# A gradient intermediate kept out of DRAM, transposes moved to other stages, and stores moved to another engine, in a fused forward and backward of linear attention and SwiGLU

## The chip, the cores and the metric

The kernel runs on one core of a Trainium2 chip. The metric is the device time of one execution in microseconds (us). Each time below is a median of several executions, and each ratio has a 95% interval. A single profile is one execution; in this case executions of one kernel differ by up to 3%, so a profile is used to see where time goes and the medians and ratios to say how much.

## The reference

One block on an input of 2048 rows and 640 columns in bfloat16, with 32 heads of 20 columns and a feed-forward width of 1728. The kernel returns the output and the gradients of x, wqkv, wo, w_gate, w_up and w_down for a given gradient of the output.

```python
def _A_ref(x, wqkv, wo):                        # linear attention
    q, k, v = ...                               # from x @ wqkv, per head
    phi = lambda t: where(t > 0, t + 1, exp(t)) + 1e-6
    pq, pk = phi(q), phi(k)
    kv  = einsum("bhsd,bhse->bhde", pk, v)
    z   = einsum("bhsd->bhd", pk)
    num = einsum("bhqd,bhde->bhqe", pq, kv)
    den = einsum("bhqd,bhd->bhq", pq, z)[..., None] + 1e-6
    return merge_heads(num / den) @ wo

def _B_ref(x, w_gate, w_up, w_down):            # SwiGLU
    return (silu(x @ w_gate) * (x @ w_up)) @ w_down

h   = x + _A_ref(layernorm(x), wqkv, wo)
out = h + _B_ref(layernorm(h), w_gate, w_up, w_down)
# ... and the vector-Jacobian product of out with grad_out
```

## The kernel before

Everything is done in row tiles of 128 rows. The parts that the argument needs, in order of time:

* **The h1 stage.** h1 = x + attention, its layer norm (`hn`) and its transpose (`hnT`). The products dm = grad_out @ w_down^T for the feed-forward gradient are computed between the others; those of three of the four column groups of w_gate and w_up are stored in DRAM.
* **Four column groups** of 448, 448, 448 and 384 columns, called groups 0 to 3. In each, g and u are computed, then m = silu(g)*u and the gradients dgate and dup (`dd`), then the weight gradients (`ps_dw`, copied out of PSUM as `dwev`). Each tile of `dd` is transposed by SP into one of three staging buffers `stg` and stored in DRAM by GpSimd. I call this the staging ring.
* **The dhn stage** reads the transposed tiles back (`cols`), **the dxn stage** makes the gradients of q and k, and the last stage makes the output from m transposed.

```python
# ... in column group g, for each pair of row tiles:
for c in range(2):                                       # the staging ring
    stg = small.tile([P, 7, P], BF16, name="stg", tag="stg", bufs=3)
    nc.sync.dma_start_transpose(out=stg[:, :GK[g], :], in_=ddt[:, tt + c, 0:2 * w])
    nc.gpsimd.dma_start(out=scr_dT[t + c, :, KO[g]:KO[g] + GK[g], :], in_=stg[:, :GK[g], :])
# ... (cut) the dm of the next group is loaded from DRAM, wgT transposed by SP
def dw(parts, copy, first=False):                        # weight gradients
    ps = mm("ps_dw")
    # ... (cut) 16 matmuls for each part
    ev = fw("dwev")
    copy(out=ev[:, :len(parts), :w], in_=ps[:, :len(parts), :w])
    for c, (_, _, dst) in enumerate(parts):
        nc.gpsimd.dma_start(out=dst[:, GO[g]:GO[g] + w], in_=ev[:, c, :w])
# ... (cut) last stage: m is transposed where it is used
def load_mT(t):
    if t % 4 == 0:
        mTs[t // 4] = strips.tile([P, 4, FT, P], BF16, name="mT", tag="S")
    nc.sync.dma_start_transpose(out=mTs[t // 4][:, t % 4], in_=scr_m[t * P:(t + 1) * P, :])
```

## Time and profile before

| | before |
|---|---|
| median of six runs beside the changed kernel | 852.02 us (847.09 to 854.31) |
| profiled span | 848.7 us |
| PE busy | 827.0 us, 97% |
| PE's two long waits | 5.4 us (at 254 us), 5.0 us (at 664 us) |

How to read it: a busy PE at its pace leaves only the waits to win, and the prediction shows them. One more line matters later, which the prediction did not use. It is from the page's part on DMA: the packets, the bytes and the mean rate over the span.

```profile
DMA packets 304402, 175.78 MB, mean 207 GB/s; under 512 B 250528, under 2 KB 290000, under 8 KB 304336
```

The five DMA queues of the page add up to 88% of the time of the 16 DMA engines. So the DMA engines are the second-busiest thing in this kernel, although no wait of PE shows it directly.

### The profile page before, as it was taken

The page shows a single profiled execution, that of the slowest core. Times are in us where ns is not written, and L with a number is a line of the kernel's source. Part 1 is how long each engine was busy: PE and PEld are TensorE (multiplying, and loading weights), DVE is VectorE, ACT ScalarE, POOL GpSimd, SP SyncE. Part 2 cuts the span into 40 slices and gives each one's busy share as a digit, 9 for nine tenths or more (in the row PEclk, how much of TensorE's full clock was granted, in tenths as well). Part 3 has the DMA queues.
Part 4 walks back from the last instruction along what each step waited for, and adds up shares of the span by engine and source line. Part 5 has one row for each costly group of instructions (what it writes and reads, how often), then busy time and mean ns, then how long its engine had stood idle before and what let it go on. Part 6 is the DMA issues. An engine that isn't in the chain of part 4 may idle for free.

```text
span 848.7 us, 14059 instructions
## 1 busy us (share of the span) xinstructions
PE 827.0 (97%) x5509; PEld 529.8 (62%) x5509; DVE 417.5 (49%) x840; ACT 297.8 (35%) x422; POOL 193.7 (23%) x352
## 2 busy tenths in 40 slices
PE   8999999999979999999999999999999799999997
PEld 6666655654535455555556777777777577777775
DVE  6978844786008603920750145577850466521111
ACT  5983433293109304800831222232221133332000
POOL 2330111222142241214213311111101122112322
PEclk9999999999999999999999999999999999999999
DMA  9999978999999995999488679567499899899692
GB/s 297 194 294 286 273 191 248 217 179 242 249 213 227 219 232 148 203 239 227 114 230 240 246 216 194 152 158 174 94 217 262 169 179 172 156 200 253 183 210 87
DMA packets 304402, 175.78 MB, mean 207 GB/s; under 512 B 250528, under 2 KB 290000, under 8 KB 304336
## 3 DMA queue, kind: packets, MB, share of 16 engines
q1 hardware_dynamic: 267808, 86.35, 53.6%
q0 software_dynamic: 19072, 70.79, 26.8%
q10 hardware_dynamic: 17456, 17.75, 7.5%
q8 instruction: 43, 0.70, 0.4%
q14 instruction: 23, 0.19, 0.1%
HBM read 53.72 MB, written 64.01 MB: 139 GB/s over the span
## 4 chain that ended last, share of the span: by engine, by line
PE 60%; DMA 16%; DVE 12%; issue 8%; POOL 1%; ACT 1%; SPq 0%; DVEq 0%; POOLq 0%; ACTq 0%
PE ps_dw L521 14%; PE ps_dxn L746 8%; PE ps_o L794 7%; PE ps_dm L315 7%; DMA dwd<-scr_dwdT 6%; PE ps_dhn L120 4%; DMA stg<-dd 4%; PE ps_kq L120 3%; PE ps_dwqk L120 3%; PE ps_y L120 3%; PE ps_a L120 3%; DMA scr_dT<-stg 2%; PE ps_dk L120 2%; PE pg L461 2%; PE pu L466 2%
## 5 line engine op out<-in xcount | busy, mean ns | idle before, releaser
L120 PE MATMUL ps_dhn<-wgT,cols 128*128 128x320 bf16 x864 | 119.5, 299 | 0.0
L521 PE MATMUL ps_dw<-dd,hn 128*128 128x448 bf16 (+1 forms) x640 | 118.8, 346 | 0.0
L120 PEld LDWEIGHTS <-cols 128*128 128x128 bf16 x864 | 84.5, 98 | 32.9
L521 PEld LDWEIGHTS <-hn 128*128 128x128 bf16 x640 | 62.6, 98 | 54.2
L523 DVE CAST dwev<-ps_dw 128x896 bf16<-128x896 f32 (+3 forms) x12 | 10.9, 908 | 140.3 <-PE ps_dw L521 82.9
L523 ACT CAST dwev<-ps_dw 128x896 bf16<-128x896 f32 (+1 forms) x20 | 17.5, 879 | 166.5 <-PE ps_dw L521 139.3
L493 POOL DMA_DIRECT2D scr_dT<-stg x64 | 34.6, 541 | 169.2 <-DMA stg<-dd 163.7
L461 PE MATMUL pg<-wgu,hnT 128*128 128x448 bf16 (+1 forms) x320 | 65.5, 352 | 6.2 <-DVE dwev L523 5.4
L466 PE MATMUL pu<-wgu,hnT 128*128 128x448 bf16 (+1 forms) x320 | 63.6, 346 | 0.0
L794 PE MATMUL ps_o<-wd,mT 128*128 128x320 bf16 x448 | 62.6, 299 | 0.0
L315 PE MATMUL ps_dm<-wdT,dh2T 128*128 128x448 bf16 (+1 forms) x320 | 62.0, 346 | 0.0
L521 PE MATMUL ps_dw<-m_s,dh 128*128 128x448 bf16 (+1 forms) x320 | 60.7, 346 | 0.9 <-DVE m_s L488 0.9
L746 PEld LDWEIGHTS <-ring 128*128 128x128 bf16 x480 | 47.0, 98 | 18.2
L794 PEld LDWEIGHTS <-mT 128*128 128x128 bf16 x448 | 43.8, 98 | 17.0
L461 PEld LDWEIGHTS <-hnT 128*128 128x128 bf16 x320 | 31.7, 99 | 34.7 <-issue 7.4
L746 PE MATMUL ps_dxn<-wqkvT,ring 128*128 128x320 bf16 x320 | 51.3, 299 | 0.0
L521 PEld LDWEIGHTS <-dh 128*128 128x128 bf16 x320 | 31.3, 98 | 28.3 <-issue 1.4
L466 PEld LDWEIGHTS <-hnT 128*128 128x128 bf16 x320 | 31.4, 98 | 27.2 <-issue 0.2
L120 PE MATMUL ps_kq<-wqk,xnT 128*128 128x320 bf16 x320 | 47.5, 305 | 0.8 <-ACT xnT L242 0.8
L315 PEld LDWEIGHTS <-dh2T 128*128 128x128 bf16 x320 | 31.3, 98 | 25.1
L120 PEld LDWEIGHTS <-xn_r 128*128 128x128 bf16 x320 | 31.8, 99 | 18.1 <-issue 5.2
L797 DVE TENSOR_TENSOR h1r<-ps_o,h1r 128x640 bf16<-128x640 f32 x15 | 12.4, 824 | 57.0 <-PE ps_o L794 54.1
(158 smaller groups left out, 1257.6 us busy)
## 6 DMA issues: line engine op xcount, KB each, us to landing
cols<-scr_dT POOLq DMA_DIRECT2D x7, 1728.0 KB, 8.6
scr_dT<-stg POOLq DMA_DIRECT2D x48, 224.0 KB, 3.3
scr_m<-m_s POOLq DMA_DIRECT2D x12, 448.0 KB, 5.1
scr_dm<-dmst ACTq DMA_DIRECT2D x16, 224.0 KB, 3.2
dm_s<-scr_dm ACTq DMA_DIRECT2D x2, 1792.0 KB, 12.4
out_dram<-dwev POOLq DMA_DIRECT2D x30, 112.0 KB, 4.6
scr_dT<-stg POOLq DMA_DIRECT2D x16, 192.0 KB, 3.0
scr_xn<-xn SPq DMA_DIRECT2D x4, 640.0 KB, 5.1
```

The source lines that it names most:

```text
L120: nc.tensor.matmul(ps[:, ci, :320], lhsT=lhs(k), rhs=rhs(k, n0, n1), start=(start and k == 0), stop=(stop and k == n - 1))
L315: nc.tensor.matmul(ps[:, c, :w], lhsT=dh2T[:, kt, (t + c) * P:(t + c + 1) * P], rhs=wdT[g // 2][:, kt, o:o + w], start=(kt == 0), stop=(kt ...
L461: nc.tensor.matmul(pg[:, c, :w], lhsT=hnT[:, kt, (t + c) * P:(t + c + 1) * P], rhs=wg[:, kt, 0:w], start=(kt == 0), stop=(kt == DT - 1))
L466: nc.tensor.matmul(pu[:, c, :w], lhsT=hnT[:, kt, (t + c) * P:(t + c + 1) * P], rhs=wg[:, kt, w:2 * w], start=(kt == 0), stop=(kt == DT - 1))
L493: nc.gpsimd.dma_start(out=scr_dT[t + c, :, KO[g]:KO[g] + GK[g], :], in_=stg[:, :GK[g], :])
L521: nc.tensor.matmul(ps[:, c, :w], lhsT=lhs(t), rhs=rhs(t), start=(t == 0), stop=(t == ST - 1))
L523: copy(out=ev[:, :len(parts), :w], in_=ps[:, :len(parts), :w])
L746: nc.tensor.matmul(ps[:, ci, :320], lhsT=lhs[:, i, :], rhs=rhs[:, i, n0:n1], start=(k == 0 and i == 0), stop=(k == 2 and i == DT - 1))
L794: nc.tensor.matmul(pss[ci][:, ci, :320], lhsT=mT[:, t % 4, j, :], rhs=wd[:, j, n0:n1], start=(j == 0), stop=(j == FT - 1))
L797: nc.vector.tensor_tensor(out=half(h1r[:]), in0=row(ps), in1=half(h1r[:]), op=ALU.add)
```

## The change

The intent, as its author put it: no dm through DRAM; late weights, phi(k) and half of m transposed into DRAM while the DMA engines idle; VectorE in emission order in the backward half. The core of the diff, with cuts:

```diff
-    scr_dm, scr_dm_v = dram_tm("scr_dm", F)
+    scr_wgT = dram.tile([P, 13, D], BF16, name="scr_wgT")
+    scr_mT = dram.tile([ST, P, 7, P], BF16, name="scr_mT")
+    scr_pkT = dram.tile([ST, P, DT, P], BF16, name="scr_pkT")
...  # W2 is transposed ahead of the h1 loop, through the staging buffers
+        for i in range(DT):
+            w2t = stage()[:, :DT, :]
+            nc.sync.dma_start_transpose(out=w2t, in_=W2[:, i, :])
+            nc.gpsimd.dma_start(out=mat_v(scr_W2T)[:, :, i * P:(i + 1) * P], in_=w2t)
...  # dm of groups 2 and 3 is made in PSUM where it is used
+                if g < 2:
+                    dmv = dm_t[g][:, t:t + 2, :w]
+                else:
+                    pdm = mm("pdm")
+                    dm_mm(pdm, wdT, t, g)
+                    dmv = pdm[:, :, :w]
...  # more work for the ring, placed between the weight gradients
+        def tr_m_dram(t):
+            stg = stage()
+            nc.sync.dma_start_transpose(out=stg[:], in_=scr_m[t * P:(t + 1) * P, 0:7 * P])
+            nc.gpsimd.dma_start(out=scr_mT[t], in_=stg[:])
+            elif g == 2:
+                side = [(tr_wgT_dram, (gg, kt)) for gg in (2, 3) for kt in range(DT)]
+                side += [(tr_m_dram, (t,)) for t in range(0, 8)]
+            else:
+                load_cols(0, act_load)
+                act_load(wgT[1][:], scr_wgT[:])
+                side = [(tr_m_dram, (t,)) for t in range(8, ST)]
...  # weight-gradient stores
-                    nc.gpsimd.dma_start(out=dst[:, GO[g]:GO[g] + w], in_=ev[:, c, :w])
+                    nc.scalar.dma_start(out=dst[:, GO[g]:GO[g] + w], in_=ev[:, c, :w])
...  # dhn stage: phi(k) transposed into DRAM; its first plain loads come before the store of GT
+            if t < ST:
+                stg = stage()
+                nc.sync.dma_start_transpose(out=stg[:, :DT, :], in_=scr_pk[t * P:(t + 1) * P, :])
+                nc.gpsimd.dma_start(out=scr_pkT[t], in_=stg[:, :DT, :])
...  # last stage: half of m comes ready from DRAM
-            nc.sync.dma_start_transpose(out=mTs[t // 4][:, t % 4], in_=scr_m[t * P:(t + 1) * P, :])
+            nc.gpsimd.dma_start(out=mTs[t // 4][:, t % 4, 0:7], in_=scr_mT[t])
+            nc.sync.dma_start_transpose(out=mTs[t // 4][:, t % 4, 7:FT], in_=scr_m[t * P:(t + 1) * P, 7 * P:FT * P])
```

## The prediction

> **What bounds the kernel now.** I read the busy table first, then the list of waits of the matmul engine, then the timeline around its two long waits, then the chain that ended last. The busy table and the clock line of the slices:
>
> ```profile
> PE 827.0 (97%) x5509; PEld 529.8 (62%) x5509; DVE 417.5 (49%) x840; ACT 297.8 (35%) x422; POOL 193.7 (23%) x352
> PEclk9999999999999999999999999999999999999999
> ```
>
> PE is busy 97% of 848.7 us. A busy PE need not be at its pace, so I checked that in the chain: ten matmuls of 448 columns take 1.89 us and ten of 320 take 1.36 us wherever they follow each other, and every stage runs so. What is left to win is only the time in which PE stands. The list of PE's waits, whole (total us, times, longest):
>
> ```profile
> PE pg L461 <- DVE dwev L523: 5.4, 1, 5.4
> PE ps_dwqk L120 <- DVE tk L731: 5.0, 1, 5.0
> PE ps_t L241 <- DVE xn L237: 2.0, 2, 1.1
> PE ps_warm L271 <- POOL ident masks.py:199: 1.4, 1, 1.4
> PE ps_dw L521 <- DVE m_s L488: 0.9, 2, 0.7
> PE pg L461 <- DMA hnT<-hn: 0.8, 1, 0.8
> PE ps_kq L120 <- ACT xnT L242: 0.8, 1, 0.8
> ```
>
> Two waits matter, and each slows the work after it. In the timeline of PE (start, length, idle before):
>
> ```profile
> 254.16 3.74 PE L461 MATMUL pg<-wgu,hnT 128*128 128x448 bf16 x10 [5.40 <-DVE dwev L523]
> 664.50 5.82 PE L120 MATMUL ps_dwqk<-dq,xn_r 128*128 128x320 bf16 x32 [5.01 <-DVE tk L731]
> ```
>
> Ten such pg matmuls take 2.05 us elsewhere and 32 such dwqk 4.51, so 1.7 and 1.3 us more go to a clock that is halved after the pause. The first wait is a queue: GpSimd issues the transposed dgate/dup tiles in order, each waiting for its transpose, and the weight-gradient stores stand behind the last of them. At 249 to 258 us it sends fourteen of them one after the other; until then their SBUF buffers, and so the PSUM, stay full. The timeline of GpSimd there:
>
> ```profile
> 248.58 0.54 POOL L493 DMA_DIRECT2D scr_dT<-stg  x1 [4.82 <-DMA stg<-dd]
> 249.11 0.54 POOL L525 DMA_DIRECT2D scr_dwdT<-dwev  x1
> 249.65 2.13 POOL L525 DMA_DIRECT2D out_dram<-dwev  x4
> ```
>
> Ahead of it is a staging ring of three buffers, transposed by SP and emptied by GpSimd. SP's timeline in column groups 0 and 1, then SP's longest wait:
>
> ```profile
> 193.29 50.34 SPq L492 DMA_TRANSPOSE stg<-dd  x16
> 261.86 48.18 SPq L492 DMA_TRANSPOSE stg<-dd  x16
> ```
>
> ```profile
> SPq L492 <- DMA scr_dT<-stg: 79.8, 37, 5.7
> ```
>
> The second wait is a load of phi(k) that GpSimd issued only at 651.99, behind a store, and that took almost 10 us to land.
>
> **What the Trainium skill says.** "TensorE: Matmul & The Clock Gate", Back-to-back issue gap, gives N/2.4 + 2.5 ns per warm matmul: 189 ns for 448 columns, 136 for 320. The trace agrees (1.89 and 1.36 us per ten): PE cannot go faster at this work. Its section What's actually happening has the clock halved for about 3.4 us after an idle window; the trace agrees with the 1.7 and 1.3 us above. "DMA: Bandwidth & Descriptors", Anatomy of one DMA, says that DMA engines do not wait on semaphores, the issuing sequencer does before it dispatches. The trace agrees: GpSimd stood, and everything behind. The same page, Issuing engines are not separate DMA queues: moving an issue to another engine saves no bandwidth, so the ring's pace does not change by that.
>
> **The change, part by part.**
> 1. *PE.* The dm products of column groups 2 and 3 (80 matmuls of 448 and 80 of 384: 15.1 + 13.0 = 28 us) move from the h1 stage into the backward groups. The number of matmuls is the same. Worth: 0 by itself.
> 2. *No dm in DRAM.* Out go 24 stores of 192 or 224 KB and three loads of 1.5 to 1.8 MB (11 to 14 us each to land). While such a load was under way the ring stood: at 288 to 300 us and 363 to 372 us two transposes took about 9 us. Without it I read from SP's issues in groups 1 and 2 before those loads (261.86 to 288.31, 337.18 to 363.56) a pace of 26 us per 10, 2.6 us per tile instead of 2.8 to 3.3. DVE reads dm of two groups from PSUM in two of its seven products. It needs 824 ns for 640 columns from PSUM against 491 from SBUF, so some 1.15 us for 896 instead of 0.62: per pair of row tiles 5 x 0.54 + 2 x 1.15 = 5.0 us beside 3 x 1.89 = 5.67 us of PE. Hidden.
> 3. *Weight-gradient stores issued by ACT.* They no longer stand behind the ring on GpSimd. This should take away the 5.4 + 1.7 us.
> 4. *phi(k) loaded early, from the staging buffers; phi(k) transposed in the idle stage; DVE in emission order.* In the changed order of GpSimd the first two phi(k) loads now stand before the stores of GT and of dwqk. This should take away 5.0 + 1.3 us.
> 5. *Small ones:* w2t leaves the path of hnT and of the ring (0.8 us), and DVE is less behind at the end of groups (0.9).
> Sum that can go: 5.4 + 1.7 + 5.0 + 1.3 + 0.8 + 0.9 = 15.1 us, or 1.8%. More there is not: the other waits are the start, and the last 5.3 us after PE are untouched.
> 6. *Added:* 10 wgT, 16 m and 16 phi(k) tiles go through the ring and DRAM, about 8.4 MB written and read back. They are not on PE, but they lengthen the ring: 16 + 18 steps in group 2, 16 + 8 in group 3.
>
> **The rivals: what takes the place of the waits.**
> *(a) ACT now stands instead of GpSimd.* In the order of the changed kernel with its waits, DMAs of SP and of ACT share eight completion semaphores in turn, and each issue waits for the user before it. So ACT's stores wait for SP's transposes, and ACT evicts PSUM in the same order. In group 1 the last stores wait for the load of the last w_gate/w_up slice, which waits for five transposes, a load, and five more. From the start of that group: first tile at 1.9 + 3 x 0.92 + 7 x 0.54 = 8.5 us; 15 steps of 2.6 = 39; five wgT transposes and landing 13 to 15 (11.45 us in the same place before, plus 3); load issue 1; five more 12 to 13; issue and landing 6. Sum 80 to 83 us. PE comes there after 30.3 + 45.4 = 75.7 us, and PSUM gives it some 4.7 more: 80.4. **So 0 to 3 us of standing, and every 0.1 us of the ring's step is 1.5 us.** At the old step of 3.2 it would be 10.
> *(b) The same in group 2.* The last store waits for ring step 32: first tile at 10.1, 31 steps of 2.6 to 2.8, 4 to land: 95 to 101 us, against 90.8 + 4.1 = 94.9 on PE. 0 to 6 us.
> *(c) The second column load of the next stage.* GpSimd issues it after all 24 ring stores of group 3, and cols(0), wgT and pqs (1.8 + 2.1 + 2.6 MB) load meanwhile; two such loads slowed the ring by 20 us before. I expect the issue some 83 us after the start of the group and the landing 9 to 15 later; PE needs it at 92. 0 to 6 us; before, it landed at 481.80 for a start at 484.4.
> *(d) The h1 stage becomes DVE's.* PE now spends 2.3 us per row tile there instead of 3.0, DVE also about 2.3. 0 to 3 us, mostly hidden by PSUM.
> *(e) Nothing takes the place.* Then the time is 852 - 15 = 837. For it speaks that the DMA bytes fall on the stages with least of them; against it that (a) to (c) are all within a few us of binding.
>
> **Range and chances.** Middle values: (a) 2, (b) 2, (c) 3, (d) 1, halved clock after them 1: 9 us. 852 - 15 + 9 = **846 us**. The low end is (e), 837, where a new wait everywhere is absent. For the high end, a ring at its old step gives 10 in (a), about 8 in (b) and less in (c), 22 in all: 859. Faster by over 2% needs less than 835, more than all that I count: 4%. Slower by over 2% needs over 869, that is 32 us of new waits: 6%.
>
> **What will show it.** The 5.4 us wait for dwev and the 5.0 us wait for tk are gone from PE's list, PE's busy us stay near 827, and DVE's products with dm from PSUM take 1.1 to 1.2 us. SP's 16 ring transposes in group 1 take 38 to 42 us. If (a) holds, PE's list has new waits of its first pg and pu matmuls in groups 2 and 3 on ACT's dwev, and ACT waits there for DMAs of the wgu, wgT or stg tiles. If (c) holds, ps_dhn waits for cols. The prediction is wrong upward if the ring's step stays above 3 us or DVE's fixed order makes it wait in the last half, and downward if the ring runs at 2.4 or less and nothing new appears.

## The result, and the profile after

| | before | after |
|---|---|---|
| median of six runs | 852.02 us | 880.12 us (868.85 to 886.08) |
| ratio | | 1.0301, interval 1.0231 to 1.037 |
| profiled span | 848.7 us | 876.0 us |

A ratio here is the mean time of one kernel's fast runs over the mean time of the other's fast runs of the same rounds, so it is not quite the ratio of the medians. The changed kernel is 3% slower, and the prediction was wrong: 880 us lies far outside its range.

The page of the changed kernel: the busy table, the clock by slices, and the DMA line.

```profile
PE 835.8 (95%) x5509; PEld 532.4 (61%) x5509; DVE 433.4 (49%) x840; ACT 284.4 (32%) x406; POOL 205.1 (23%) x366
PEclk9999989999999999997999899999899999999999
DMA packets 292483, 181.76 MB, mean 207 GB/s; under 512 B 239840, under 2 KB 276512, under 8 KB 292288
```

PE has the same 5509 matmuls but is busy 8.8 us longer: this is halved clock. The mean clock that PE was granted is 0.981 against 0.992 before, and the clock line has slices below 9 where before it had none. The transfers have 6 MB more.

PE's list of waits in the changed kernel (total us, times, longest), its seven longest:

```profile
PE pg L474 <- ACT dwev L546: 7.0, 2, 6.9
PE ps_dhn L122 <- DMA cols<-scr_dT: 6.2, 1, 6.2
PE ps_dhn L122 <- ACT dwev L546: 6.1, 1, 6.1
PE ps_a L122 <- DVE xr L424: 5.5, 1, 5.5
PE ps_dp L122 <- DMA dh1T<-dh: 2.6, 1, 2.6
PE ps_t L245 <- DVE xn L241: 2.0, 2, 1.1
PE pu L479 <- ACT m_s L497: 1.6, 1, 1.6
```

Both waits of before are gone. In their place stand five others of more than 2 us. The sum closes within 1 us: new are 7.0 + 6.2 + 6.1 + 5.5 + 2.6 + 1.6 us, 0.9 us for a tile `ring<-dq` and 0.7 us for h1r, together 30.6 us; PE's busy time adds 8.8; gone are 5.4 + 5.0 + 0.8 = 11.2. That makes 28.2 us, and the spans differ by 27.3.

The wait at the end of group 2, in the chain that ended last (start, length, what):

```profile
388.74 4.80 DMA stg<-scr_m
...
395.11 4.96 DMA scr_mT<-stg
...
400.08 4.91 DMA stg<-scr_m
...
405.01 0.02 ACTq L552
```

Right after it ACT empties the PSUM of the weight gradients and PE goes on at 406.40. The reader sees one staging buffer going round: an m tile is transposed in 4.8 us, stored in 5.0, and only then does the next m tile take the buffer. ACT's store waits for that next tile, although it has nothing to do with it. In the program of the changed kernel, DMAs issued by SP and by ACT share eight completion semaphores in turn, so an issue waits for the earlier DMA that holds its semaphore. ACT's next eviction (its copy of finished sums out of PSUM) stands behind the store, and PE behind the eviction. The ring in groups 2 and 3, in SP's timeline (start, length):

```profile
315.56 40.02 SPq L510 DMA_TRANSPOSE stg<-dd  x16
355.67 29.53 SPq L456 DMA_TRANSPOSE stg<-wgu  x10
387.42 22.82 SPq L462 DMA_TRANSPOSE stg<-scr_m  x8
413.98 49.63 SPq L510 DMA_TRANSPOSE stg<-dd  x16
463.70 29.25 SPq L462 DMA_TRANSPOSE stg<-scr_m  x8
```

The ring of group 2 ends at 410 us, while PE stops at 399.5, a few tiles into group 3. In group 3 the ring ends at 493; PE is through with the group at 482.

The wait in the h1 stage, in GpSimd's timeline:

```profile
119.19 1.74 POOL L413 DMA_DIRECT2D scr_W2T<-stg  x2 [10.99 <-DMA stg<-yk]
120.97 0.24 POOL L133 TENSOR_SCALAR lnv<-mv 128x1 f32<-128x1 f32 x1
121.29 0.57 POOL L134 TENSOR_TENSOR rstd<-lnv,nhalf 128x1 f32<-128x1 f32 x1
```

GpSimd stands 11 us on the last transposed tiles of W2, with the small operations of the layer norm behind them in its order; PE stands for them from 117 us.

### The profile page after: what moved, and what is told of

Same layout as the page of the kernel before. It is cut to its first block, busy times and chain, and to the rows that moved or that the text cites. A ratio compares the mean times of both kernels' runs of the same rounds, so it can differ in the third digit from the quotient of the medians.

```text
span 876.0 us, 14086 instructions
## 1 busy us (share of the span) xinstructions
PE 835.8 (95%) x5509; PEld 532.4 (61%) x5509; DVE 433.4 (49%) x840; ACT 284.4 (32%) x406; POOL 205.1 (23%) x366
## 2 busy tenths in 40 slices
DMA packets 292483, 181.76 MB, mean 207 GB/s; under 512 B 239840, under 2 KB 276512, under 8 KB 292288
## 3 DMA queue, kind: packets, MB, share of 16 engines
q1 hardware_dynamic: 258400, 85.96, 51.3%
q0 software_dynamic: 20496, 78.87, 30.5%
## 4 chain that ended last, share of the span: by engine, by line
PE 54%; DMA 23%; DVE 11%; SPq 5%; issue 3%; ACT 2%; POOL 1%; ACTq 0%; DVEq 0%; POOLq 0%
PE ps_dhn L122 12%; PE ps_dxn L784 7%; PE ps_o L832 6%; DMA stg<-dd 5%; PE ps_dw L544 5%; PE ps_dwqk L122 4%; PE ps_kq L122 3%; PE ps_y L122 3%; DMA scr_dT<-stg 2%; PE ps_dk L122 2%; PE pg L474 2%; PE pu L479 2%; PE pdm L313 2%; SPq L581 2%; PE ps_dm L313 2%
## 5 line engine op out<-in xcount | busy, mean ns | idle before, releaser
L122 PE MATMUL ps_dhn<-wgT,cols 128*128 128x320 bf16 x864 | 124.5, 307 | 12.3 <-DMA cols<-scr_dT 6.2
L122 PEld LDWEIGHTS <-cols 128*128 128x128 bf16 x864 | 86.4, 100 | 48.7 <-DMA cols<-scr_dT 6.6
L784 PE MATMUL ps_dxn<-wqkvT,ring 128*128 128x320 bf16 x320 | 51.3, 299 | 0.9 <-DMA ring<-dq 0.9
L501 DVE TENSOR_TENSOR m_s<-m_s,dd 128x896 bf16<-128x896 bf16 (+1 forms) x32 | 19.3, 603 | 49.7 <-ACT m_s L497 49.7
L495 ACT ACTIVATE dd<-pg 128x896 bf16<-128x896 f32 (+1 forms) x32 | 28.6, 893 | 36.6 <-PE pg L474 34.4
```

Of the source, the lines that this page charges most:

```text
L122: nc.tensor.matmul(ps[:, ci, :320], lhsT=lhs(k), rhs=rhs(k, n0, n1), start=(start and k == 0), stop=(stop and k == n - 1))
L495: nc.scalar.activation(out=dg, in_=pg[:, :, :w], func=ACT.Sigmoid)
L501: nc.vector.tensor_tensor(out=m, in0=m, in1=dg, op=ALU.mult)
L784: nc.tensor.matmul(ps[:, ci, :320], lhsT=lhs[:, i, :], rhs=rhs[:, i, n0:n1], start=(k == 0 and i == 0), stop=(k == 2 and i == DT - 1))
```

## The experiments

The first theory, T1, was that the loss is the sum of separate new waits, each with its own part of the change, and that the gains are real. Eighteen kernels were run, all with a correct result, each against the kernel before in the same rounds. "The changed kernel" is the one with the whole change.

### 1. One part of the change undone

**W2 transposed behind the h1 loop again (w2t_late).**

```diff
-        for i in range(DT):
-            w2t = stage()[:, :DT, :]
-            ...
+    for i in range(DT):          # behind the h1 loop, in a buffer of the work pool
+        w2t = wk("w2t")
+        ...
```

> The changed kernel with the transposing of W2 moved back behind the h1 loop and into its old buffers, nothing else. Theory (T1): the loss of 28 us is the sum of separate new waits, and the first of them, 5.5 us of PE on xr at 117 us plus about 3.4 us of halved clock, comes because GpSimd stands on the transposes of W2 with the rstd operations behind it. Then the 5.5 us wait and the halved clock at 122 us go, a wait of hnT of under 1 us may come back at the end of that stage, and the time falls by 6 to 9 us, to a ratio of 1.020 to 1.024 against the kernel before. Rival (R1): VectorE, in a fixed order and with less PE work per row tile there, is what bounds this stage, and the wait only shows up there first. Then a wait of PE on xr of 3 us or more stays somewhere in the stage, and the time falls by under 3 us.

Measured: 878.32 us, ratio 1.0335 (1.0265 to 1.0405). The wait on xr is gone, but the time does not fall. In the place of one wait came three: 3.0 us of pg on ACT and 3.5 us of ps_dw on the load of `dh` behind those transposes, and the waits on `cols` grew from 6.2 to 10.2 us. T1 holds for the cause of the wait and fails for its worth. (This profile fell in a slow run of 881.8 us.)

**No half of m through DRAM (no_mT).** I call that half, seven of the fourteen blocks of each m tile, the m half.

```diff
-                side += [(tr_m_dram, (t,)) for t in range(0, 8)]
-                side = [(tr_m_dram, (t,)) for t in range(8, ST)]
-            nc.gpsimd.dma_start(out=mTs[t // 4][:, t % 4, 0:7], in_=scr_mT[t])
-            nc.sync.dma_start_transpose(out=mTs[...][:, t % 4, 7:FT], in_=scr_m[..., 7 * P:FT * P])
+            nc.sync.dma_start_transpose(out=mTs[t // 4][:, t % 4], in_=scr_m[t * P:(t + 1) * P, :])
```

> The changed kernel without the transposed half of m in DRAM: no m tiles through the staging ring in groups 2 and 3 (16 fewer ring steps), m transposed whole at the end as before. T1: ACT's stores of weight gradients stand behind the ring, so a shorter ring lets them go: the 7.0 us wait of pg at 399 us and the 6.1 us wait of ps_dhn on dwev at 482 us both fall under 2 us, with the halved clock after them (about 5 + 3.4 us); 12 to 20 us less, ratio 1.008 to 1.017. If the last stage needed the pre-transposed m, a new wait of ps_o on mT appears, 0 to 4 us. Rival (R2): not the ring's length but the coupling itself, ACT standing behind SP's transposes; the waits then stay above 4 us each and the time falls by under 5 us. Rival (R3): reading dm from PSUM makes VectorE late in group 2; then the wait at 399 us stays and that at 482 us goes.

Measured: 855.6 us, ratio 1.0075 (1.0043 to 1.0108). The profiled execution is the second fastest of its 17, with a span of 845.9 us. The busy table of its page:

```profile
PE 827.2 (98%) x5509; PEld 529.7 (63%) x5509; DVE 433.7 (51%) x840; ACT 285.2 (34%) x406; POOL 187.9 (22%) x334
```

And the two longest of PE's waits:

```profile
PE ps_a L122 <- DVE xr L424: 5.1, 1, 5.1
PE ps_dp L122 <- DMA dh1T<-dh: 4.0, 1, 4.0
```

All three waits of 6 to 7 us are gone, that of `cols` at 608 us among them, and PE's busy time is back at 827. The dm products still come from PSUM, so R3 falls. No wait on mT came at the end, so the pre-transposed half had been of no use there. This one part of the change makes some 2.2% of the 3%.

**Weight-gradient stores back on GpSimd (dw_gpsimd).**

```diff
-                    nc.scalar.dma_start(out=dst[:, GO[g]:GO[g] + w], in_=ev[:, c, :w])
+                    nc.gpsimd.dma_start(out=dst[:, GO[g]:GO[g] + w], in_=ev[:, c, :w])
```

> The changed kernel with only the stores of weight gradients given back to GpSimd. T1 (length of the ring): GpSimd's stores stand behind the same ring steps, so waits of PE at the ends of groups 2 and 3 stay, at 5 us or more each, and at the end of group 0 the old wait of some 5 us is there again; the time is within 1% of the changed kernel's, ratio 1.02 to 1.045. Rival (R2, coupling through ACT): ACT is free again to evict PSUM, the waits at 399 and 482 us fall under 2 us, and the time falls by 10 us or more, ratio under 1.02.

Measured: 881.83 us, ratio 1.0372 (1.0298 to 1.0445). As much is lost, by other ways. From PE's list of waits:

```profile
PE ps_dhn L122 <- DMA cols<-scr_dT: 12.2, 2, 6.4
PE pu L479 <- ACT m_s L497: 4.8, 1, 4.8
PE pg L474 <- DVE dd L504: 4.0, 1, 4.0
```

All three are at the ends of groups 2 and 3 or later. So the coupling of ACT to SP's ring is the form in which the loss shows, not what it needs: rival R2 falls. There is a second reading. At 245 to 258 us PE does not wait at all here, although the stores are on GpSimd as in the kernel before. T1 had expected the old wait back. The prediction gave the 5.4 us to ACT's stores (its part 3); in the changed kernel something else has removed it. The ring of group 0 is faster: its 16 transposes took 42.1 us here, 41.0 in the changed kernel and 50.3 before, and GpSimd has issued the last weight-gradient store of the group at 229 us, where in the kernel before it was still at it when PE waited at 254. What is gone from that stretch are the stores and the load of dm and the transposes of w_gate and w_up; which of them it was, no run parts.

**No staging of phi(k) (no_pkT).** The four lines in the dhn stage go, and phi(k) is transposed from DRAM in the dxn stage as before.

> The changed kernel without the staging of phi(k): no transposes and stores of it in the dhn stage; phi(k) is transposed from DRAM in the dxn stage as before. T1: in the dhn stage GpSimd stands on those transposes, so that it issues a load of cols late at 605 us; without them the 6.2 us wait of ps_dhn on cols and the halved clock after it go, perhaps the 2.6 us of ps_dp on dh1T too: 7 to 12 us less, ratio 1.015 to 1.022. The dxn stage may get back some wait for the ring of phi(k), 0 to 3 us. Rival (R4): the cols loads are late because of bandwidth or of the other loads ahead of them; then the wait on cols stays above 3 us and the time falls by under 4 us.

Measured: 877.01 us, ratio 1.0364 (1.0309 to 1.0419). The wait on `cols` keeps its 6.1 us and only moves from 608 to 499 us, and the wait of ps_dp on dh1T stays (2.4 us). T1 was wrong here: phi(k) is not what makes `cols` late. The wait and the time came as R4 had expected; whether bandwidth or the loads ahead is the reason, as R4 has it, this run does not show. In no_mT, where phi(k) is staged, `cols` is not late; with m staged and phi(k) not, it is. In the changed kernel SP issues the first transpose of dh1 at 502.6 us, after the m tiles, and in no_mT at 480.7: the dhn stage starts behind.

### 2. How much of m, and where

**The changed kernel again (after_again).**

> The changed kernel itself, once more, on the same chip as the next three. Its ratio against the kernel before should be 1.023 to 1.037 again; it is the yardstick for the three.

Measured: 873.63 us, ratio 1.029 (1.0235 to 1.0345); the yardstick stands.

**The m tiles of group 2 only, and of group 3 only (m_g2_only, m_g3_only).**

> The changed kernel with only the 8 transposes of m in group 2 kept; those in group 3 are undone, and m of row tiles 8 to 15 is transposed whole at the end. Theory (T1, each end of a group pays for the ring steps put into it): the wait of about 7 us at the end of group 2 (399 us) stays, with its halved clock; at the start of the dhn stage the wait of ps_dhn on ACT's dwev falls under 2 us, and because that stage then does not start behind, the wait of ps_dhn on cols near 608 us goes as well. Time 12 to 19 us under the changed kernel, ratio 1.010 to 1.020. Rival (R5, the debt is carried on): what is late after group 2 stays late, the waits at 482 and 608 us stay at 4 us or more each, ratio 1.02 or more.

> The changed kernel with only the 8 transposes of m in group 3 kept; those in group 2 are undone. T1: the wait at 399 us falls under 2 us; the waits of ps_dhn on ACT's dwev at about 480 us and on cols later stay at 4 us or more each (together 10 to 13 us with some 7 us of halved clock). Ratio 1.012 to 1.024. R5: if the waits at 482 and 608 us came from the debt of group 2, they fall under 2 us each and the ratio is under 1.012.

The waits are of PE, in us, from the profile of each.

| m tiles staged | median us | ratio | waits at end of group 2 | waits at 470 to 500 us | cols near 600 us |
|---|---|---|---|---|---|
| both groups (after_again) | 873.63 | 1.029 | 4.8 | 12.9 | 4.6 |
| group 2 only | 868.31 | 1.0256 (1.0200 to 1.0311) | 4.6 | 0 | 0 |
| group 3 only | 866.61 | 1.0233 (1.0187 to 1.0280) | 0 | 4.2 | 2.2 |
| none (no_mT) | 855.6 | 1.0075 (1.0043 to 1.0108) | 0 | 0 | 0 |

(after_again was profiled in a slow run; no_mT was run in other rounds, on another chip.) Each group's own end pays for the steps put into it, and the late `cols` goes with those of group 3: this is T1 in kind, and R5 (a debt carried from group 2) falls. In size the waits of group 3 only are smaller than T1 had expected (2.4 us on dwev, 1.8 and 2.2 on `cols`, where it had 4 or more each). The ratio with group 2 only lies above what was expected, that with group 3 only within it, and the times are not a sum, as T1 would have them. Half of the tiles costs 1.6 to 1.8%, all cost 2.2%, and with half of them other waits came, among them 2.5 us on a tile of the dxn ring and 3.2 us on dKV in group 2 only, and 3.5 us on h1r in group 3 only.

### 3. Repairs on top of no_mT

**W2 through free buffers, SP's order carried on (no_mT_h1_sp).** W2 is transposed at the same place into buffers of another pool, GpSimd stores it in the middle of the h1 loop, and the dhn stage and the next form one block in SP's order.

```diff
-            w2t = stage()[:, :DT, :]
+            w2t = fw("w2t")...           # free between the first stage and group 0
-            nc.gpsimd.dma_start(out=mat_v(scr_W2T)[...], in_=w2t)
+                if 6 <= t < 6 + DT:      # inside the h1 loop
+                    nc.gpsimd.dma_start(out=mat_v(scr_W2T)[...], in_=w2ts[t - 6])
```

> The changed kernel without the m half in DRAM, and with two repairs: W2 is transposed at the same place but into free buffers of another pool, and GpSimd stores it in the middle of the h1 stage, so that no rstd operation stands behind it; and SP keeps its emission order from the dhn stage into the next, so that the last transpose of dh1 goes ahead of the 15 of w_qkv. T1: the 5.1 us wait on xr near 117 us and the 4.0 us wait of ps_dp on dh1T near 619 us go, each with 1.7 to 3.4 us of halved clock; no new wait over 2 us; 10 to 14 us under the version without the m half, ratio 0.990 to 0.998 against the kernel before. Rival (R1): VectorE bounds the h1 stage; then a wait of 3 us or more on xr stays there, and the ratio is 0.998 to 1.004.

Measured: 854.65 us, ratio 1.0059 (1.0029 to 1.009). The two waits went as expected, on xr near 117 us (4.4 us in several small waits of 1.2 us or less are left in that stage, which VectorE now bounds) and on dh1T. New are 4.8 us of ps_dk on the transposes of WV2, which now stand behind 15 of w_qkv in SP's order, and 3.2 us on `cols`. A gain of 0.2% lies within the intervals.

**Another order of SP (no_mT_h1_sp2).**

> As the version without the m half and with the two repairs, but the ten transposes of the other two thirds of w_qkv come after those of WV2 in SP's order. T2: the 4.8 us wait of ps_dk on WK2 near 658 us and its halved clock go, that of cols (3.2 us) may stay; ratio 0.994 to 1.001. Rival (R11: SP has too much to do there, whatever its order): a wait of 3 us or more of ps_dxn or ps_dk on ring or wqkvT tiles takes its place, ratio 1.002 or more.

In this version ten of the fifteen w_qkv transposes go behind those of WV2. Measured: 857.84 us, ratio 1.0123 (1.0074 to 1.0173). The wait on WV2 is gone, and 7.1 us of ps_dk on ACT and 7.6 us on `cols` are there. T1 failed in the first repair and T2 (section 4 names it) in the second: each change of SP's order made something else late. The second ratio is R11's, but the waits are not on the tiles that R11 named.

### 4. One part of the change alone, in the kernel before

> The kernel before with one part of the change alone: the weight-gradient stores issued by ACT. The prediction counted 5.4 us of wait and 1.7 us of halved clock as what this part can take away at 254 us. Theory (T1: the gains of the prediction are real, and the loss is new waits of other parts): the wait of pg on dwev at 254 us goes, no new wait over 2 us, ratio 0.990 to 0.996. Rival (R6: ACT's coupling to SP's ring costs as much as it saves, even with the old ring): waits on ACT's dwev or m_s of 3 us or more at the ends of the groups, ratio 0.998 or more.

> The kernel before with one part of the change alone: the first phi(k) loads issued early, from the staging buffers. The prediction counted 5.0 us of wait and 1.3 us of halved clock at 664 us. T1: the wait of ps_dwqk on tk goes, ratio 0.991 to 0.997. Rival (R7: something else is as late at that place, the transposes of WV2 or the loads of xnT): a wait of 3 us or more of ps_dk or ps_dwqk on another tile takes its place, ratio 0.998 or more.

> The kernel before with both of these parts. T1: both waits go, ratio 0.982 to 0.992, that is 7 to 15 us less: the two gains add up, and the version beats both kernels. R6 and R7: one or both replaced, ratio 0.994 or more.

| kernel before and ... | edit | median us | ratio |
|---|---|---|---|
| b_act | weight-gradient stores on ACT | 857.07 | 1.0145 (1.0083 to 1.0206) |
| b_pk | phi(k) loaded early into the ring's buffers | 862.8 | 1.0191 (1.0131 to 1.0251) |
| b_act_pk | both | 870.92 | 1.0289 (1.0231 to 1.0347) |

All three miss T1. With them T1 falls as a sum of parts. For b_act, first a line of PE's waits:

```profile
PE ps_dw L521 <- ACT dwev L523: 13.2, 3, 7.1
```

Then one of ACT's:

```profile
ACT dwev L523 <- DMA stg<-dd: 83.3, 4, 35.3
```

The wait at 254 us is gone, but ACT stands 35 us on the ring in group 0, and PE 13.2 us on ACT. The ring runs until 240 us there; moving the stores only changed who stands behind it. This is R6.

b_pk says little on its question. The 5.0 us wait of ps_dwqk on tk is gone, but the edit was clumsy: the loads went into the ring's own buffers and stood in GpSimd's order ahead of weight-gradient stores of group 3, and PE waited 11.2 us for those. So the loads were tried again in other buffers. From here on the theory is T2: the ring's added steps cost because of where they stand, and a gain is real where nothing else is touched.

```diff
+        pkrs = {}
+        def load_pk(t):
+            pkrs[t] = wk("pkr", pool=1)
+            nc.gpsimd.dma_start(out=pkrs[t][:], in_=scr_pk_v[:, t, :])
+        load_pk(0)
+        load_pk(1)
         GT = mat("GT")               # its store follows in GpSimd's order
```

This is b_pk2.

> The kernel before with the first phi(k) loads issued before the store of GT, into their old buffers; the clean form of the last test. Theory (T2: the gain is real where nothing else is touched): the 5.0 us wait of ps_dwqk on tk and its 1.3 us of halved clock go, the rest of the list stays as before, ratio 0.991 to 0.996. Rival (R7: another transfer is as late at that place): a wait of 3 us or more of ps_dk, ps_dwqk or ps_dxn takes its place, ratio 0.997 or more.

Measured: 844.39 us against 848.39, ratio 0.9944 (0.9916 to 0.9972), over 22 and 27 runs. It is the only version that beats both kernels. From its list of PE's waits (the profile fell in a slow run of 851.2 us):

```profile
PE ps_dwqk L120 <- DVE tk L731: 2.4, 1, 2.4
```

The wait halved instead of going, and the ratio is worth 4.8 us of 848.

**The m half alone, added to the kernel before (b_m)**, its weight-gradient stores left on GpSimd:

```diff
+            side = []
+            if g >= 2:
+                side = [(tr_m_dram, (t,)) for t in range(8 * (g - 2), 8 * (g - 1))]
...
                 copy(out=ev[:, :len(parts), :w], in_=ps[:, :len(parts), :w])
+                if side:
+                    f, args = side.pop(0)
+                    f(*args)
```

> The kernel before with the m half through DRAM added and nothing else: 8 more ring steps in each of groups 2 and 3, weight-gradient stores still on GpSimd. Theory (T2: the longer ring alone is enough): new waits of PE at the ends of groups 2 and 3, on dwev or cols, of 4 us or more each, ratio 1.012 to 1.03. Rival (R9: it needs the other parts of the change as well, ACT's stores or the weights in the same ring): new waits under 3 us in all, ratio under 1.008.

Measured: 885.79 us, ratio 1.0481 (1.043 to 1.0533), more than T2 expected. The two waits of PE that stand for it:

```profile
PE ps_dhn L121 <- DMA cols<-scr_dT: 13.9, 1, 13.9
PE pu L473 <- ACT u L487: 6.9, 1, 6.9
```

Other waits grew with them, among them 7.9 us on h1r in the last stage and 7.9 on tk. So the m half is necessary for most of the loss (no_mT), and in the kernel before it makes a loss of more than the whole (b_m); R9 falls.

**No staging at all (no_staging)**: W2, m and phi(k) as before, the rest of the change kept.

> The changed kernel with all three stagings undone together: W2 back behind the h1 loop, m and phi(k) transposed where they are used. Left of the change are dm kept out of DRAM, the last two slices of w_gate/w_up through DRAM, ACT's stores, the early phi(k) loads and VectorE's order. T1: of the list of PE's waits nothing over 3 us is left but dh1T (4 us), ratio 0.985 to 0.998. Rival (R8: the parts that are left, dm from PSUM and the late weights, cost as well): ratio 0.999 to 1.01, with waits of pg, pu, ps_dw or ps_dhn of 3 us or more.

Measured: 857.29 us, ratio 1.0113 (1.0054 to 1.0173), not below that of no_mT. T1 failed, and the ratio lies a little above R8's range. Of its longest waits, 3.7 us are of ps_dw, which R8 named, but on the load of `dh` behind the transposes of W2 as in w2t_late, and 3.7 us on the ring of dk; neither is dm or the late weights. What holds this version back was not found.

### 5. What in the m half costs: its place, its bytes or its steps

**The same 16 transposes in the dhn stage (m_late)**, behind those of phi(k).

> The changed kernel with the 16 transposes of the m half moved out of groups 2 and 3 into the dhn stage, behind those of phi(k); as many tiles go through the ring and DRAM as in the changed kernel. Theory (T2: the steps cost because of where they stand): the waits at 399 and 482 us fall under 2 us; the dhn stage has 16 more steps in SP's and GpSimd's order, so waits of ps_dhn on cols or of ps_dp on pqr or dh1T of 3 to 8 us in all come there; ratio 1.008 to 1.020. Rival (R10: m through DRAM costs by its traffic, wherever it is): waits of as much as in the changed kernel in the dhn stage or on mT at the end, ratio 1.022 or more.

Measured: 879.83 us, ratio 1.0377 (1.0322 to 1.0433). The ends of groups 2 and 3 are free of waits, as T2 expected, but the dhn stage pays more than it expected, and the ratio is in R10's range. The longest wait (the profile fell in a slow run of 884.9 us; 11.7 us of ps_dp on dh1T stand beside it):

```profile
PE ps_dhn L122 <- DMA cols<-scr_dT: 16.1, 1, 16.1
```

GpSimd's timeline shows the load of `cols` issued at 592.26 us, behind stores that each wait for a transpose, when PE was ready for it at 590.7. The load landed at 606.8, after 14.5 us where these loads take 9.3 in the median, and the DMA engines are 93% busy in that stretch (475 to 610 us). So in this profile both take part: order, as T2 has it, in the late issue, and, as R10 has it, probably traffic in the slow landing. The next two runs part bytes from steps.

**The same steps with a seventh of the bytes (m_one)**: each m tile of seven blocks of 128 columns is cut to one, and the other thirteen blocks of m are transposed at the end.

```diff
-            nc.sync.dma_start_transpose(out=stg[:], in_=scr_m[t * P:(t + 1) * P, 0:7 * P])
-            nc.gpsimd.dma_start(out=scr_mT[t], in_=stg[:])
+            nc.sync.dma_start_transpose(out=stg[:, 0:1, :], in_=scr_m[t * P:(t + 1) * P, 0:P])
+            nc.gpsimd.dma_start(out=scr_mT[t, :, 0:1], in_=stg[:, 0:1, :])
```

> The changed kernel with each of the 16 staged m tiles cut from seven blocks of 128 columns to one: the same 16 transposes, 16 stores and 16 loads in the same order through the same buffers, with a seventh of the bytes; the other thirteen blocks are transposed at the end. Theory (T2: steps in SP's and GpSimd's order cost): the waits on dwev near 399 and 482 us stay at 3 us or more each, ratio 1.020 or more. Rival (R10: the bytes cost, in DMA engines that are busy 87% of the span already): these waits fall to under 2 us each, ratio 1.005 to 1.014, about that of the version without the m half. In between: both.

Measured: 857.83 us, ratio 1.0114 (1.007 to 1.0157). This is what R10 had expected, in the ratio and in the waits; T2, with 1.020 or more, failed. So the number of steps is not what costs. SP's timeline of the two series of m steps:

```profile
380.50 16.04 SPq L462 DMA_TRANSPOSE stg<-scr_m  x8
...
450.76 24.87 SPq L462 DMA_TRANSPOSE stg<-scr_m  x8
```

A step takes 2.0 us in group 2 instead of 2.85, and 3.1 instead of 3.7 in group 3. The ring of group 2 now ends at 396.5 us and PE does not wait there; in group 3 1.8 us of ps_dhn on dwev are left. A seventh of the bytes still takes most of a step's time. The Trainium skill, "DMA: Bandwidth & Descriptors", section Anatomy of one DMA, gives a fixed cost of about 2.0 us per DMA on GpSimd's path; the trace agrees for small ones: the store of an m tile lands after 2.0 us (median) with 32 KB, after 3.0 us with 224 KB.

**The same bytes without the steps (traffic)**: no m half; GpSimd instead copies 16 times 2 x 224 KB of m from DRAM to an unused place in DRAM, in groups 2 and 3.

```diff
+            r, c = (t + 8, 448) if t < 8 else (t, 832)
+            for k in range(2):
+                nc.gpsimd.dma_start(out=scr_tf[t, k], in_=scr_m[r * P:(r + 1) * P, c:c + 896])
```

> The changed kernel without the m half, but with 32 copies of 224 KB from m in DRAM to an unused place in DRAM, 16 at the end of group 2 and 16 in group 3, issued by GpSimd: as many bytes in these groups as the transposes and stores of the m half, no step in the ring, none on SP. R10: PE waits at the ends of groups 2 and 3 of 5 us or more in all, ratio 1.015 to 1.035. T2: waits of under 3 us in all, ratio 1.004 to 1.012. Caution: such copies have longer rows than a transpose, so they may take less DMA time for the same bytes.

Measured: 851.64 us, ratio 1.0027 (1.0002 to 1.0051). PE has no wait over 0.2 us at the ends of groups 2 and 3: T2's side of this test, with a ratio a little under its range. The page's DMA line, and in the view by stretches the one of group 2 (us, PE, PEld, DVE, ACT, POOL, granted clock, DMA share, GB/s):

```profile
DMA packets 291970, 181.74 MB, mean 214 GB/s; under 512 B 239328, under 2 KB 276000, under 8 KB 291776
```

```profile
316.00:398.00 82.00, 82.00 (x439) 42.66 (x438) 37.08 (x52) 25.94 (x32) 29.27 (x46) 1.00 0.96 229
```

It moves as many bytes as the changed kernel (181.76 MB), the DMA engines are 96% busy in group 2, more than in the changed kernel in the same stretch (89%), and PE is busy all the 82 us. **In the column groups bytes outside the ring do not cost; R10 falls there**, with the caution that these copies need less DMA time per byte than transposes. They do slow the ring: SP issues its last transposes of groups 2 and 3 at 392.4 and 453.1 us, but PE comes to where it would stop at 399.3 and 472.4.

m_one and traffic, each taken alone, seem to contradict each other. What fits both is the time for which the steps hold the ring: a transpose, a store and the hand-over between SP and GpSimd, eight of them in a row, at a place with little room. The bytes count as far as they lengthen a step. How little room there is, SP's timeline of no_mT shows, in groups 2 and 3:

```profile
353.49 30.02 SPq L456 DMA_TRANSPOSE stg<-wgu  x10
399.80 44.58 SPq L510 DMA_TRANSPOSE stg<-dd  x16
```

SP is through with the ring of group 2 at 383.5 us and of group 3 at 444.4, and PE comes to where it would stop at 396.0 and 469.1. Into these 12 and 25 us, less the landing of the last tile, the changed kernel puts m steps of 22.8 and 29.3 us; m_one puts 16.0 and 24.9 there and keeps 1.8 us of wait. This account is worked out from one profile of each; no run changed the room alone.

## Why the prediction was wrong

By its own steps:

* **What bounds the kernel**: right. PE's matmuls stayed at their pace, and in the profile the loss is waits of PE and the halved clock behind them.
* **Part 1** (the dm products move, worth 0): nothing contradicts it; it was not tried alone. **Part 2** (no dm in DRAM): right on the operations; DVE's products from PSUM took 1.08 us (expected 1.15), 16 transposes of group 1 took 43.3 us (expected 38 to 42, so 2.7 a step), of group 2 40.0 us. The faster ring in group 0, to which this part may add, is what dw_gpsimd points to for the 5.4 us wait, in place of part 3.
* **Part 3** (ACT's stores take away 5.4 + 1.7 us): the wait went, but it is gone without this part too (dw_gpsimd), so that this came true was luck. Alone in the kernel before, the part costs 1.45% (b_act).
* **Part 4** (phi(k) early, 5.0 + 1.3 us): right in kind. Alone, in a clean form and without VectorE's order, it is worth 4.8 us.
* **Part 5** (W2 leaves the path, 0.8 us): wrong in sign. The wait of hnT went, and 5.5 us of ps_a came, because GpSimd has the layer norm's operations behind the new stores.
* **Part 6** and its rivals are the step that failed: what the added tiles cost. It said that the added tiles "lengthen the ring" and are "not on PE", and let rivals (a), (b) and (c) carry the cost: 2 + 2 + 3 us, at most 22 with (a) at a slow ring. Term by term against the profile after: (a) 2, measured 1.6; (b) 2 in a range of 0 to 6, measured 7.0; (c) 3, measured 0 on `cols` at that place but 6.1 us on ACT's dwev, which stands behind the m tiles of group 3 as in (b), and which no rival named; (d) 1, measured 5.5 us, by GpSimd's order and not by VectorE's work; halved clock 1, measured 8.8 more net of the 3.0 that went; not foreseen at all, 6.2 us on `cols` at 608 and 2.6 us on dh1T. It had 9 us in all; the profile has 30.6 us of new waits and 8.8 us of clock.
* **In (b) the pace was nearly right and the start was not.** The prediction had the first ring tile of group 2 at 10.1 us after PE's start there, then steps of 2.6 to 2.8 us, and 4 us to land. Measured: the first tile is issued at 14.2 us (301.37 to 315.56), because ACT, still behind its stores of group 1, began with the group only at 308.5 us. This is rival (a), which was added up apart from (b). The tile for which ACT's store waits is the 31st, issued at 400.08: 2.8 us a step. It lands after 4.9. Within the ring the steps differ: 2.5 us for the first 16, about 3.2 for a weight tile (355.67 to 387.42 for ten), 2.85 for an m tile, and 3.1 and 3.7 for a tile of dd and of m in group 3.
* **The chance of 6% for "slower"** came from adding 32 us of new waits as if that were an extreme. The working listed four places within a few us of binding; in this profile each of the four new waits of 5 us and more is followed by halved clock, and it counted none of the follow-on waits. So 859 was too low an upper end.

What is shown: the m half is the cause of about 2.2% of 3% (no_mT), and alone it makes the kernel before slower too (b_m). In the column groups it costs through the time that its steps add to the ring; their number alone (m_one) and as many bytes beside the ring (traffic) cost little or nothing. What stays open: no_mT is still 0.75% above the kernel before, though the gains of part 4 should put it below. The size of that rest is not sharp: traffic, which is no_mT with copies added, came out at 1.0027 in other rounds on another chip. The waits on W2 and dh1T account for that in its profile (5.1 + 4.0 us), but two repairs of them brought other waits and no certain gain, and no_staging was no better. I take from this only that the fixed orders of SP and GpSimd have no room at several places; which order would keep the gain was not found.

## What to carry to other kernels

When work is moved off a busy engine into a "hidden" chain, write down when that chain ends and when its user comes, stage by stage; a chain with 12 us to spare has no room for eight steps of 3 us, whatever else is free. Count for every in-order issuer what stands behind each new wait: here a store of W2 stopped a layer norm, and a weight gradient's store waited for a transposed tile of m. Try the parts of a change one at a time: here a small one, two loads issued earlier, was the only one with a proven gain (0.9944), and in the whole change it could not be seen.

## What the Trainium skill lacked or had wrong

* "DMA: Bandwidth & Descriptors" (Issuing engines are not separate DMA queues) counts only the time on the sequencer as the worth of another issuing engine. It lacks that moving issues can cost: with the stores on ACT alone, ACT stood 83.3 us in four waits on SP's transposes, and the ratio was 1.0145.
* "Advanced Engine Details and Errata" (X-Bar Transpose (TRN2)) calls transposing DMAs as fast as regular ones and puts them at about 90% of a copy's bandwidth. In the changed kernel SP's queue, with all the transposes and some plain loads, took 51.3% of the engines' time for 85.96 MB, GpSimd's queue with plain transfers 30.5% for 78.87 MB: 5.2 against 3.4 us per MB (share x 876.0 us over MB), which is 65%. This is the packets' time in a busy mix; no run timed a transpose alone.
* No page read for this case has the time of a staged step, that is a transpose into SBUF by one engine and a store by another through three buffers: 2.5 to 3.1 us for a tile of dd, 2.85 to 3.7 for a tile of m out of DRAM, and still 2.0 to 3.1 with a seventh of its bytes.
